# Turned first-tile blocks, token sums on VectorE, a last row block in three sums and a new stored order, in a two-block attention kernel

## The chip, the cores and the metric

The kernel runs on one core of one Trainium2 chip. The metric is the device time of one launch in microseconds (us). The names of the engines are those of the profile: PE is TensorE, DVE is VectorE, ACT is ScalarE, POOL is GpSimd and SP is SyncE. SP and ACT each have a hardware queue on which they start transfers, and POOL has a software queue.

## The reference

Two blocks share the shapes S = 2048 tokens, D = 640 features, H = 32 heads of Dh = 20, all in bf16. Block A is causal attention in a sliding window of 256 tokens, block B is linear attention with a feature map.

```python
# A
q, k, v = split_heads(x @ wqkv)
scores = einsum("bhqd,bhkd->bhqk", q, k) * Dh ** -0.5
mask = (i - j >= 0) & (i - j < 256)
p = softmax(where(mask, scores, -1e9))
a = merge_heads(einsum("bhqk,bhkd->bhqd", p, v)) @ wo
# B
phi = lambda t: where(t > 0, t + 1, exp(t)) + 1e-6
pq, pk = phi(q), phi(k)
kv = einsum("bhsd,bhse->bhde", pk, v)
z = sum of pk over the tokens s
num, den = pq @ kv, pq . z + 1e-6
b = merge_heads(num / den) @ wo
return concatenate([a, b], axis=-1)
```

The output has 2048 rows of 1280 columns, A's 640 and then B's 640.

## The kernel before

**How the order comes about.** The program records every piece of work as an operation of a planner: what it emits, on which engines it can run, what it waits for, and which shared buffer it takes. Nothing is decided at run time. The list `SEQ` (L17) holds the order: each word is an operation's number times 8 plus an engine, and `follow` (L204) emits the operations in that order. One list therefore fixes at once the order on each engine and on each queue, and the engine of each eviction that could run on ACT or on DVE.

**Shared buffers.** PSUM is split into one four-bank buffer S for scores and four one-bank buffers F0 to F3 for all other products. Four row tiles in SBUF (O0 to O3, the tile `osb`) collect rows of 640 columns before a store; a row tile comes free when its store has landed. The buffers `K0` to `K3` hold the mapped keys `pk` of the four token tiles of B and later the mapped queries `pq`; `T0` to `T3` hold the tokens of B and later `kvwo` and small sums.

**Block A.** The tokens are taken in four tiles of 512 (t = 0 to 3). A tile comes in turned, features on the partitions, by one DMA of 512 rows (`load_x`, L553). The first tile is different: its four blocks of 128 rows come in as they are (`x0n`, L1209), and PE turns each with five transposes into one PSUM buffer (L1242), which one copy moves to SBUF. `proj` makes queries and keys (512-column matmuls at L577), and POOL's DMAs at L608 and L611 regroup them into the tiles `even` and `odd`. `proj_v` makes the values (320-column matmuls, L638), and DMAs on SP's queue make the swapped copy `sw`. The weights `wq` and `wk` come in as five rows of tiles each and are copied by ACT or DVE into a padded form (L484, L486), one copy for each and a sixth for the rest.

Attention goes by score units: 16 to 24 small matmuls fill S (L708), one exponential on ACT takes S to the tile `p` (L724), DVE multiplies the edges of the window by a 0/1 strip (L736). Four units of tile 0 or five units of a later tile make a group of 8 heads; then the products with the values follow (PV, L764), 32 columns at a time, and the two result buffers are copied to `ost` and written to DRAM (L786). There are 4 groups a tile and 76 units in all. The values carry a column of ones, so the sums of the softmax come out as rows of the same product. `a_out` reads results (`oc`, L825) and sums (`osum`, L829) back, takes 1/sum as an exponential of a logarithm, scales on DVE, and multiplies by `woA` in `finish_rows` (L792): for a block of 128 rows two sums of five 320-column matmuls (L798), two copies into a row tile, and one store of 128 x 640 (L812).

**Block B.** `b_keys` makes keys from token tiles (320-column matmuls, L913), and `phi_evac` maps them: an exponential on ACT (L874), a min-and-add and a max on DVE (L878, L881). `b_sums` makes the product of tokens and mapped keys over all 16 blocks of tokens (L938), so that kv follows from it with the value weights (L1037) and, with `wo`, the matrix `kvwo` (L1055), which goes through DRAM (`kvd`, stores through row tiles). `b_z` makes the token sums of `pk`: 32 matmuls with a tile of ones of 32 columns (L974) sum over the partitions and over the four blocks of a tile; two copies and two subtractions (L986, L989) split the sums into a high and a low bf16 part, and small matmuls with a constant 1/32 turn them into columns, from which DVE makes `Zc` (L1002). `b_query` makes the mapped queries (512-column matmuls, L1107), the denominators (20 matmuls of 128 columns, L1125), their reciprocals on ACT (L1132, L1138), a spreading DMA (`recB`, L1146), the scaling on DVE (L1171), and the output by `finish_rows` with `kvwo`.

**The ends of the run.** At the start `heat` (L1185) issues 20 matmuls on a zeroed tile `warm` and four times two more. The table of ACT's functions is loaded before everything else (L505), with one small exponential (L509). At the end the last row blocks of B (named ob3.0 to ob3.3) go out. After all that a guard follows, which would compute A in a slower general form if a softmax sum left a range; here it is skipped.

## Time and profile before

| | before |
|---|---|
| median of 3 runs | 250.89 us (250.74 to 251.39) |
| the profiled run's own time | 250.49 us |
| span of the profiled execution | 248.8 us |
| busy: PE, ACT, DVE, POOL | 239.9, 200.8, 172.6, 40.4 us |
| PE busy with weight loads (beside matmuls) | 144.3 us |
| moved by DMA | 36.61 MB, mean 147 GB/s |

The span goes from the first to the last recorded instruction of the profiled execution; the run's own time holds what lies around it too. A row of the timeline has the start in us, the length, the engine, the line, the operation, out <- in by the program's names, the shape, and how often it was repeated without a break. A number in square brackets is the idle time ahead of it and what ended it. In the chain of waits each row is one step back from the last instruction. The ends of matmuls are modelled, so starts are surer than lengths.

### The profile page before, as it was taken

The numbers are of one execution on the slowest core, as the hardware profiler recorded it, in microseconds if no ns is written. First come the engines' busy times: TensorE is split into PE (matmuls) and PEld (weight loads), VectorE is DVE, ScalarE is ACT, GpSimd is POOL, SyncE is SP. The second block draws the span as 40 slices with busy tenths as digits, with TensorE's granted clock in tenths as the row PEclk, the third lists the DMA queues.
The fourth block names the chain that finished last, engine by engine and source line by source line (L and its number), as shares of the span: only waits on it lengthen the run. The fifth ranks groups of instructions, "written<-read, shape, count | busy, mean of one in ns | idle before, by whom it ended". The sixth has DMA issues, their size and how long they took to land.

```text
span 248.8 us, 9643 instructions
## 1 busy us (share of the span) xinstructions
PE 239.9 (96%) x4167; PEld 144.3 (58%) x4193; DVE 172.6 (69%) x441; ACT 200.8 (81%) x222; POOL 40.4 (16%) x93
## 2 busy tenths in 40 slices
PE   7999999999999999999999999999989999999993
PEld 6644565454655666545566666666555665565671
DVE  2553587778679978886666363369999899949740
ACT  2459898988999999988998788789999987946532
POOL 6003460063002601004078000000000000000000
PEclk9999999999999999999999999999999999999999
DMA  6999226649364759913573768863545472236433
GB/s 216 284 148 243 59 66 148 154 90 166 87 223 111 198 99 213 277 42 72 143 194 75 124 154 258 202 164 105 159 139 151 119 167 84 76 114 186 135 128 111
DMA packets 54216, 36.61 MB, mean 147 GB/s; under 512 B 34249, under 2 KB 52761, under 8 KB 54169
## 3 DMA queue, kind: packets, MB, share of 16 engines
q1 hardware_dynamic: 50537, 31.52, 49.7%
q0 software_dynamic: 2048, 2.63, 5.3%
q10 hardware_dynamic: 1584, 1.80, 2.2%
q8 instruction: 33, 0.54, 1.0%
q14 instruction: 14, 0.11, 0.2%
HBM read 13.90 MB, written 10.26 MB: 97 GB/s over the span
## 4 chain that ended last, share of the span: by engine, by line
PE 87%; ACT 6%; DVE 3%; issue 2%; DMA 1%; ACTq 0%; DVEq 0%
PE F L577 17%; PE F L798 16%; PE S L708 10%; PE F L638 9%; PE F L913 9%; PE F L938 9%; PE F L764 6%; PE F L1107 5%; ACT p L724 4%; DMA out_dram<-osb 1%; PE F L1185 1%; DVE pq L881 1%; PE F L1037 1%; ACT e L874 1%; PE F L1242 1%
## 5 line engine op out<-in xcount | busy, mean ns | idle before, releaser
L724 ACT ACTIVATE p<-S 128x2048 bf16<-128x2048 f32 x76 | 141.1, 1856 | 16.4 <-PE S L708 14.5
L736 DVE TENSOR_TENSOR p<-p,strip 128x256 bf16<-128x256 bf16 (+2 forms) x140 | 49.4, 381 | 21.1 <-ACT p L724 20.5
L874 ACT ACTIVATE e<-F 128x320 bf16<-128x320 f32 (+1 forms) x52 | 25.5, 501 | 8.3 <-PE F L1107 5.8
L638 PE MATMUL F<-wv,xT 128*128 128x320 bf16 x160 | 31.7, 300 | 0.1
L913 PE MATMUL F<-wkB,xT 128*128 128x320 bf16 x160 | 30.7, 299 | 0.2 <-issue 0.2
L798 PE MATMUL F<-woA,oc 128*128 128x320 bf16 x160 | 30.3, 300 | 0.0
L611 POOL DMA_DIRECT2D odd<-st x32 | 18.2, 573 | 69.3 <-ACT st L484 28.8
L577 PE MATMUL F<-xT,wk 128*128 128x512 bf16 x91 | 27.8, 380 | 0.3
L577 PE MATMUL F<-xT,wq 128*128 128x512 bf16 x92 | 26.9, 380 | 0.5 <-issue 0.3
L938 PE MATMUL F<-pk,xtok 128*128 128x320 bf16 x160 | 27.1, 300 | 0.0
L798 PE MATMUL F<-kvwo,pq 128*128 128x320 bf16 x160 | 25.9, 300 | 0.9 <-DVE pq L1171 0.4
L1107 PE MATMUL F<-xT,wqB 128*128 128x512 bf16 x91 | 25.4, 381 | 0.3
L486 DVE CAST ost<-F 128x512 bf16<-128x512 f32 x26 | 17.1, 685 | 10.2 <-PE F L764 10.0
L486 DVE CAST even<-F 128x512 bf16<-128x512 f32 x24 | 16.5, 688 | 8.2 <-PE F L577 7.9
L486 DVE CAST osb<-F 128x320 bf16<-128x320 f32 x33 | 15.5, 486 | 8.6 <-PE F L798 7.9
L608 POOL DMA_DIRECT2D odd<-even x32 | 16.6, 524 | 25.4 <-DVE even L486 23.2
L764 PE MATMUL F<-p,vt 64*32 64x320 bf16 (+4 forms) x720 | 20.5, 253 | 0.0
L638 PEld LDWEIGHTS <-xT 128*128 128x128 bf16 x160 | 15.1, 98 | 9.2 <-issue 1.3
L913 PEld LDWEIGHTS <-xT 128*128 128x128 bf16 x160 | 15.0, 98 | 8.9 <-issue 1.2
L764 PE MATMUL F<-p,sw 64*32 64x320 bf16 (+3 forms) x720 | 19.9, 253 | 0.2 <-DVE kvs L486 0.2
L798 PEld LDWEIGHTS <-pq 128*128 128x128 bf16 x160 | 14.9, 98 | 8.7 <-issue 1.6
L484 ACT CAST osb<-F 128x320 bf16<-128x320 f32 x31 | 12.6, 426 | 8.5 <-PE F L798 6.2
(85 smaller groups left out, 295.8 us busy)
## 6 DMA issues: line engine op xcount, KB each, us to landing
OD<-ost SPq DMA_DIRECT2D x32, 128.0 KB, 2.2
out_dram<-osb SPq DMA_DIRECT2D x24, 160.0 KB, 2.1
oc<-OD SPq DMA_DIRECT2D x4, 640.0 KB, 4.9
xtok<-in_B_x_dram SPq DMA_DIRECT2D x4, 640.0 KB, 4.5
odd<-even POOLq DMA_DIRECT2D x32, 48.0 KB, 2.9
sw<-vt SPq DMA_DIRECT2D x16, 87.0 KB, 3.1
out_dram<-osb ACTq DMA_DIRECT2D x8, 160.0 KB, 2.1
odd<-st POOLq DMA_DIRECT2D x32, 32.0 KB, 3.1
```

Source lines behind the costliest of these rows:

```text
L486: nc.vector.tensor_copy(out=dst, in_=src)
L577: nc.tensor.matmul(ps[:, a:b], lhsT=w[:, kt, i, :], rhs=xb["t"][:, kt, a:b], start=(kt == 0), stop=(kt == KT - 1))
L638: return lambda ps: nc.tensor.matmul(ps[:], lhsT=xb["t"][:, kt, bb * P : bb * P + P], rhs=rhs_(), start=(kt == 0), stop=(kt == KT - 1))
L708: nc.tensor.matmul(st["s"][64 * i : 64 * i + 64, o0 : o0 + b - a], lhsT=kb["t"][32 * j : 32 * j + Dh, sl, ko : ko + 64], rhs=qb["t"][32 * ...
L724: nc.scalar.activation(out=o_, in_=i_, func=ACT.Exp, scale=scale)
L736: nc.vector.tensor_tensor(out=x, in0=x, in1=mkv[:, None, :].to_broadcast([P, 4, 64 * w]), op=ALU.mult)
L764: nc.tensor.matmul(O[i][32 * j : 32 * j + 32, a:b], lhsT=lhsT, rhs=pb["t"][64 * i : 64 * i + 64, o0 + js * j : o0 + js * j + b - a], start ...
L798: return lambda ps: nc.tensor.matmul(ps[:], lhsT=lhs(c), rhs=rhs(c, hf), start=(c == 0), stop=(c == KT - 1))
L874: nc.scalar.activation(out=eb["t"][:, 0:n], in_=ps[:], func=ACT.Exp)
L913: return lambda ps: nc.tensor.matmul(ps[:], lhsT=xb["t"][:, kt, b * P : (b + 1) * P], rhs=R["wkB"][:, kt, hf * HALF : (hf + 1) * HALF], st ...
L938: return lambda ps: nc.tensor.matmul(ps[:], lhsT=R["xt", tb // 4][:, tb % 4, c * P : (c + 1) * P], rhs=R["pk", tb // 4][:, tb % 4, hf * HA ...
L1107: return lambda ps: nc.tensor.matmul(ps[:], lhsT=R["wqB"][:, kt, :].rearrange("p (f c) -> p c f", c=KT)[:, c, :], rhs=xb["t"][:, kt, :], s ...
```

## The change

- **First loads.** Blocks 2 and 3 of the first tile of A come in turned, by two DMA transposes of 128 rows on SP's queue, ahead of the loads of `wk` and `wq`. Blocks 0 and 1 are still turned on PE. The load of block 0 stays first on SP's queue; that of block 1 is now the first on ACT's queue, ahead of `wv0`, `wv2` and `wv4`. The first tile's SBUF layout goes by block, so that a turned block lies in one piece. The load of ACT's table and the small exponential become an operation of the order, after the copy of the first turned block. The fillers read a constant tile of ones that needs no memset; there are 18 and 16 small ones first, then two times two.
- **Token sums.** The 32 matmuls with ones and the four operations on their PSUM sums go. DVE adds up the 16 blocks of `pk` in a f32 tile of 128 x 640 (15 additions, each waiting for the one before and for its block), then splits it into high and low parts; the partitions are summed by the small matmuls that were there, with ones in place of 1/32. `Zc` moves into the tile of the parts.
- **Row tiles.** `K2` and `K3`, free of keys once the parts are made, serve as two more row tiles from there on. Until then two `hold` operations, which emit nothing, keep them taken.
- **Last row block.** ob3.2, the last in the new order, is summed in 320, 160 and 160 columns, and stored in two pieces, 480 columns and 160.
- **Weight loads of B.** `wkB`, `wvB` and `wqB` come in two transfers each, three fifths and two fifths.
- **Fillers at the first denominators.** 40 matmuls of 8 columns go ahead of the 20 of den0, into columns of the same buffer that nothing reads.
- **Order.** `SEQ` is replaced as a whole, and PV takes the pieces of its units in the order given for tile 0, in pairs of long and short for the others.

```diff
-PRM = {"sq": "SP", "dens": 4}
+PRM = {"sq": "SP", "dens": 4, "nwarm": 18, "pad": 4, "nfill": 2, "xT0": 2, "dpad": 10, "wsplit": 1, "lastb": 2}
 SEQ = [
...
+    XO = {"OK2": "K2", "OK3": "K3"} if PRM.get("xo", 1) else {}
+    pl = Planner(FB + ["S0"] + list(XO) + [f"O{i}" for i in range(PRM.get("nosb", 4))] + ["L0"])
+    held = [{} for _ in XO]
+    for g_ in held:
+        pl.op({"SP": 1}, lambda e: None, -(10 ** 8), [], name="hold", slots=(1, "O"), g=g_)
...
+    WSP = [(0, 3), (3, 5)] if PRM.get("wsplit") else [(0, 5)]
...
-        warm = mk("o", [P, NQ], BF16, "warm", tag="L0")
-        nc.vector.memset(warm[:], 0.0)
-        nc.scalar.preload_act_table_set("natural_log_exp_and_others")
+        warm = nc.const_aps.tensor(1.0, (P, P), BF16)
...
+    def row_tile(sb, name):
+        tag = sb["slot"][0]
+        return mk("over", [P, D], BF16, name, tag=XO[tag]) if tag in XO else mk("o", [P, D], BF16, name, tag="osb" + tag)
...
-        for hf in range(2):
+        cuts = [(0, HALF), (HALF, 480), (480, D)] if last else [(0, HALF), (HALF, D)]
+        for k, (a, b) in enumerate(cuts):
...
-        st = dma(lambda e: q_of(e).dma_start(out=out2[tb * P : (tb + 1) * P, col0 : col0 + D], in_=sb["t"][:]), D_STORE, -4000, ends, name="store")
+        for a, b, need in [(0, 480, ends[:2]), (480, D, ends[2:])] if last else [(0, D, ends)]:
+            st = dma(lambda e, a=a, b=b: q_of(e).dma_start(out=out2[tb * P : (tb + 1) * P, col0 + a : col0 + b], in_=sb["t"][:, a:b]), (340, 1, int(420 * (b - a) / D), 350), -4000, need, name="store")
...
-                        nc.tensor.matmul(ps[hf][32 * s : 32 * s + 32, :], lhsT=ones[:], rhs=R["pk", s][:, b, hf * HALF : (hf + 1) * HALF], start=(b == 0), stop=(b == 3), tile_position=(0, 32 * s), skip_group_check=True)
...
+        for k in range(1, NT):
+            def add(e, k=k):
+                if "zacc" not in R:
+                    R["zacc"] = mk("const", [P, D], F32, "zacc")
+                blk = lambda i: R["pk", i // 4][:, i % 4, :]
+                nc.vector.tensor_tensor(out=R["zacc"][:], in0=blk(0) if k == 1 else R["zacc"][:], in1=blk(k), op=ALU.add)
+            need = pk_ops[2 * k : 2 * k + 2] + (pk_ops[0:2] if k == 1 else [prev])
+            prev = pl.op({"DVE": 730}, add, 4000 + k, need, name=f"zs{k}")
+        def hi(e):
+            hl["t"] = mk("over", [P, 3, D], BF16, "hl", tag="T3")
+            nc.vector.tensor_copy(out=hl["t"][:, 0, :], in_=R["zacc"][:])
+        def lo(e):
+            nc.vector.tensor_tensor(out=hl["t"][:, 1, :], in0=R["zacc"][:], in1=hl["t"][:, 0, :], op=ALU.subtract)
...
-            nc.sync.dma_start(out=R["wqB"][:], in_=wBv[:, :, 0:D])
+            for a, b in WSP:
+                nc.sync.dma_start(out=R["wqB"][:, a:b, :], in_=wBv[:, a:b, 0:D])
...
+                for i in range(PRM.get("dpad", 0) if t == 0 else 0):
+                    for s_ in range(4):
+                        nc.tensor.matmul(dg["w"][32 * s_ : 32 * s_ + 32, 256:264], lhsT=ones[:], rhs=ones[:, 0:8], start=True, stop=True, tile_position=(0, 32 * s_), skip_group_check=True)
...
+                for i in range(b, b + n):
+                    nc.sync.dma_start_transpose(out=x0_tile()[:, i, :, :], in_=xA[i * P : (i + 1) * P, :])
...
+        def tables(e):
+            nc.scalar.preload_act_table_set("natural_log_exp_and_others")
+            tinyo = mk("const", [P, 1], F32, "tinyo")
+            nc.scalar.activation(out=tinyo[:], in_=tiny[:], func=ACT.Exp)
...
-            nc.sync.dma_start(out=x0n["t"][:, b, :], in_=xA[b * P : (b + 1) * P, :])
+                q_of(e).dma_start(out=x0n["t"][:, b, :], in_=xA[b * P : (b + 1) * P, :])
```

148 lines of the change are left out of this document (79 added, 69 removed), and 187 rows, old and new, of the table SEQ.

## The prediction

> **What bounds the kernel now.** I read the page first, then the timeline of PE between two score units, then the same between units late in the run.
>
> ```profile
> span 248.8 us, 9643 instructions
> PE 239.9 (96%) x4167; PEld 144.3 (58%) x4193; DVE 172.6 (69%) x441; ACT 200.8 (81%) x222; POOL 40.4 (16%) x93
> PE 87%; ACT 6%; DVE 3%; issue 2%; DMA 1%; ACTq 0%; DVEq 0%
> ```
>
> PE has 96% of the span and 87% of the chain that ended last, but a modelled matmul end hides short waits, so I test it by starts. Full-width matmuls that follow one another:
>
> ```profile
> 228.50 2.20 PE L798 MATMUL F<-kvwo,pq 128*128 128x320 bf16 x15
> 14.77 2.32 PE L577 MATMUL F<-xT,wq 128*128 128x512 bf16 x10
> ```
>
> The last of a row ends 0.30 (0.38) after it starts, as single ones do, so a 320-column matmul costs (2.20 - 0.30) / 14 = 0.136 us of PE and a 512-column one (2.32 - 0.38) / 9 = 0.216. Now one interval from a score unit (S, L708) to the next:
>
> ```profile
> 85.64 0.50 PE L708 MATMUL S<-odd 20*64 20x320 bf16 x16
> 86.08 1.67 PE L798 MATMUL F<-woA,oc 128*128 128x320 bf16 x11
> 87.58 0.84 PE L913 MATMUL F<-wkB,xT 128*128 128x320 bf16 x5
> 88.36 0.42 PE L708 MATMUL S<-odd 20*64 20x192 bf16 x16
> ```
>
> 16 x 0.136 = 2.18, plus 0.44 for S and 0.10 to turn back to row-tiled work, is 2.72: all of the interval. Counted so, with the instructions of the program's order, the intervals from the first unit (18.11) to the last (213.63) come out within about 0.1 us each, except three. So the kernel is bound by PE's own work, and by a second limit close under it, the loop of score unit and exponential:
>
> ```profile
> 181.83 0.43 PE L708 MATMUL S<-even 20*64 20x320 bf16 x24
> 182.37 1.88 ACT L724 ACTIVATE p<-S 128x2048 bf16<-128x2048 f32 x1
> 184.30 0.43 PE L708 MATMUL S<-even 20*64 20x128 bf16 x24 [0.54 <-ACT p L724]
> ```
>
> There is one S buffer, so the next unit waits for the exponential: 2.47 us per unit at least, while PE had only some 1.5 us of work here. An interval cannot shrink below that.
>
> ```profile
> core 0: us, PE busy (x) PEld busy (x) DVE busy (x) ACT busy (x) POOL busy (x), PEclk, DMA share, GB/s
> 113.04:165.88 52.84, 52.66 (x1123) 33.10 (x1125) 28.61 (x72) 44.89 (x40) 13.27 (x27) 1.00 0.65 159
> 165.88:176.38 10.50, 10.30 (x179) 6.48 (x181) 9.32 (x25) 9.50 (x9) 0.00 (x0) 1.00 0.40 114
> 176.38:184.30 7.92, 6.86 (x173) 4.15 (x173) 7.74 (x20) 7.82 (x9) 0.00 (x0) 1.00 0.50 164
> ```
>
> From 113 to 166 PE is full and DVE has 24 us free; from 176 to 184 DVE and ACT are full and PE waits. Those are the three exceptions: 7.92 us for about 6.1 us of PE work, 1.8 us lost.
>
> **The change part by part.** The whole order is replaced, so I counted each interval of the new order in the same way.
>
> *The start.*
>
> ```profile
> 1.50 2.74 PE L1185 MATMUL F<-warm 128*128 128x128 bf16 x24 [1.50 <-DVE tiny L507]
> 4.81 0.49 DVE L486 COPY xT<-F 128x640 bf16<-128x640 bf16 x1 [3.36 <-PE F L1242]
> 5.66 2.47 PE L638 MATMUL F<-wv,xT 128*128 128x320 bf16 x16
> 7.97 0.44 PE L1242 MATMUL F<-ident,x0n 128*128 128x128 bf16 x5
> 8.24 0.43 PE L638 MATMUL F<-wv,xT 128*128 128x320 bf16 x2
> 8.52 0.44 PE L1242 MATMUL F<-ident,x0n 128*128 128x128 bf16 x5
> 8.79 2.20 PE L638 MATMUL F<-wv,xT 128*128 128x320 bf16 x15
> 10.80 1.22 DVE L486 COPY wk<-wkn 128x512 bf16<-128x512 bf16 x5 [0.52 <-DMA wkn<-in_A_wqkv_dram]
> 9.86 4.51 SPq L553 DMA_TRANSPOSE xT<-in_A_x_dram  x1
> ```
>
> Blocks 2 and 3 of the first tile come turned by DMA: two groups of transposes leave PE, 8.24 - 7.97 and 8.79 - 8.52, so -0.54. Two fillers now stand between the first value matmuls: +0.1. The second block's load goes first on ACT's queue instead of second on SP's, three wv loads follow it there, and the filler no longer waits for a memset (1.50), so the first value matmul (5.66) can come earlier; but the first copy moves from DVE (0.49) to ACT, which by its 426 ns for 320 columns and 584 for 512 needs an estimated 0.7, behind three more DMA issues and a table load. I take -0.2. Against it: the two turned loads stand on SP's queue before all ten wk and wq loads. A 512-row turn holds SP for 4.51 us, a quarter of that is 1.1, so two take 2.3 where two plain loads took 0.9, and DVE already waited 0.52 for wk. I charge nothing more than the gain I held back above. Start: -0.6, bounds -1.1 (first matmul 0.6 earlier) and +0.8 (wk late by the 1.4 of issue, less the saved 0.6).
>
> *Token sums.*
>
> ```profile
> 166.23 1.27 PE L974 MATMUL F<-pk,ones 128*32 128x320 bf16 x32
> 167.44 1.27 PE L1107 MATMUL F<-xT,wqB 128*128 128x512 bf16 x4
> L881 DVE SCALAR_TENSOR_TENSOR pq<-F,e 128x512 bf16<-128x512 f32 x20 | 13.7, 689 | 0.6
> L881 DVE SCALAR_TENSOR_TENSOR pk<-F,e 128x320 bf16<-128x320 f32 x32 | 15.6, 490 | 0.9
> L1002 DVE TENSOR_TENSOR Zc<-blk,zs 128x640 bf16<-128x640 bf16 x1 | 0.8, 826 | 0.0
> ```
>
> PE loses 32 matmuls, 167.44 - 166.23 = -1.2. DVE gains 15 adds of 640 f32 elements. From 490 to 689 ns for 192 more is 1.04 ns an element; from 512 to 640 that makes 0.82, as the 640-wide product at L1002 has. I take 0.8 each, 12 us in all (0.5 if they ran like the bf16 products, 1.0 if f32 in SBUF costs more), less the four copies that leave. They lie in 113 to 166, where 24 us are free. The cover is thinnest where seven stand in a row, 5.6 us, ahead of the last six masks of tile 2, group 3: counted from the exponentials they depend on, the masks end about 0.3 us after the PV there could start. +0.1; without cover, 12 us.
>
> [...]
>
> *The loop's floor.* With 1.8 us less PE work before the late stage, three intervals hold 2.31, 2.33 and 2.34 us where about 2.43 is the least: +0.3.
>
> *The late stage* (units from 174 to 192). Per unit ACT has the same exponentials; other ACT work is nearly equal, and it set the pace before: 0. Forty 8-column fillers join the first denominator group, 10 to 25 ns each (weight loads of 20 such take 0.31): 0.4 to 1.0, partly in PE's wait; with two sums and the split copies DVE has about 1 us more in a stage where it is full. Together +0.3, bounds -1.0 and +1.5.
>
> *Halved weight loads:* one more SP issue each, 0.5 us, hidden by loads that are due 5 us later. *Row tiles, last block:*
>
> ```profile
> 218.97 0.48 PE L1125 MATMUL F<-pq,Zc 128*32 128x128 bf16 x20
> 222.71 0.60 ACT L874 ACTIVATE e<-F 128x512 bf16<-128x512 f32 x1 [2.41 <-PE F L1107]
> 225.89 0.58 PE L798 MATMUL F<-kvwo,pq 128*128 128x320 bf16 x3 [0.42 <-DVE pq L1171]
> 240.34 3.43 DMA out_dram<-osb
> 243.84 0.43 ACT osb L484
> 244.32 0.85 PE F L798 x5
> 245.20 0.42 ACT osb L484
> out_dram<-osb ACTq DMA_DIRECT2D x8, 160.0 KB, 2.1
> recB<-recS SPq DMA_DIRECT2D x16, 32.0 KB, 1.9
> ```
>
> The first three rows are the timeline, the next four the chain, the last two the DMA issues. At 240.34 a store holds the row tile that an eviction needs, four PSUM buffers fill, and PE waits some 0.5 before 244.32. Six row tiles instead of four end that: -0.5. The other tail wait (225.89) stays: the new order has 4.0 us of PE work from the denominator to the first product that needs it, where the old had 5.9; but its scale multiply stands two DVE results earlier. I get a wait of 0.9 where 0.6 was. Smaller tail waits even out. Tail: -0.4, bounds -1.2 and +0.8. At the end the last eviction is 160 columns, an estimated 0.29 instead of 0.42, and the last store 40 KB: by 2.1 and 1.9 above, -0.1. End: -0.2.
>
> Sum: -0.6 - 1.2 + 0.1 + 0.3 + 0.3 - 0.4 - 0.2 = -1.7. The profiled run took 250.49, that is 1.7 outside its span, and 0.40 under the median of 250.89. Off the median, with rounding, 249.1.
>
> **The rivals.** *All stalls go* (247.3): the 1.8 us of the late stage vanish too. For it: they come from DVE's order (copies of kvwo, masks), and that is new. Against: ACT's sum there is as long as before.
>
> *The turned blocks come late* (250.6): DMA is the limit of the first 10 us, SP's queue is 1.4 us longer, and wk was just in time; then start is +0.8 and more, and only the token sums pay.
>
> *VectorE becomes the bound* (slower, 252.3): the seven adds hold the masks, PV comes late, and two adds and two splits follow into the full stage. Eleven operations at c us each cost 11c - 8.8 of delay; 0.96 is break-even, at 1.1 it is 3.3. For it: no row shows an f32 add in SBUF. Against: no 640-wide row is above 0.826.
>
> *PE's clock comes up late* (250.8): the 24 fillers start 0.107 apart ((2.74 - 0.29) / 23), the transposes at 7.97 0.055, so PE runs at half rate until about 5.7. The new filler ends near 3.4 and PE may idle until the first block lands; if full rate came one filler's length (2.7) plus that later, 3.4 us of work at half rate lose 1.7. The profile's granted clock is 1.00 throughout and shows none of it. [...]
>
> **How the numbers follow.** Forecast 0.52 (248.1 to 250.2), all stalls go 0.18, late blocks 0.13, late clock 0.08, VectorE 0.09. What a measurement can tell from no change is 0.3%, 0.75 us: faster is below 250.14, slower above 251.64. Faster takes 0.50 + 0.18 + 0.06 of the late cases: 0.76; slower 0.09 and a little of the late ones: 0.10; the rest 0.14. Range 247.4 to 251.0: it leaves out the VectorE case and the lower part of the first rival.
>
> **What would show it.** First value matmul near 5.4 and first score unit near 17.5; no idle before the first key matmul. No matmuls from the ones tile on 640-wide keys; 15 adds of about 0.8; the unit before PV of tile 2, group 3 not longer than 2.8. Units from 174 to 192 still paced by the exponential. PE without a wait in its last 5 us, and the last eviction near 0.3. I am wrong if the first unit is not earlier than 18.1, if adds take 1 us, or if units of 113 to 166 exceed their matmul sum.

## The result and the profile after

| | before | after |
|---|---|---|
| median | 251.06 us (250.21 to 252.14, 18 runs) | 252.58 us (251.22 to 253.50, 18 runs) |
| profiled run, and its span | 250.49, 248.8 us | 252.12, 250.6 us |
| ratio after / before | | 1.0059, 95% interval [1.0040, 1.0078] |

The changed kernel is slower by 0.6%. The forecast of 249.1 was wrong in sign, and the range up to 251.0 did not hold the time. Runs in which the chip was in its slower state (one of a_w26d7, two of a_w26code, and one of the kernel before beside a_dpad6) are left out of the medians and ranges below.

First the page of the changed kernel: span, engines, one DMA queue, the chain that ended last.

```profile
span 250.6 us, 9689 instructions
PE 240.0 (96%) x4181; PEld 144.1 (57%) x4206; DVE 184.1 (73%) x452; ACT 202.3 (81%) x223; POOL 40.5 (16%) x92
...
q8 instruction: 34, 0.56, 1.0%
...
PE 87%; DVE 4%; ACT 3%; DMA 2%; issue 2%; ACTq 0%; DVEq 0%
```

Nothing there says what went wrong: PE has the same share, DVE has the 11.5 us of additions it was given, and the span is 1.8 us longer. So I cut the span by the starts of score units, which both kernels share (unit S1.2.3 is the fourth of group 2 of tile 1, counted from 0), and set the stretches side by side. The last two columns are experiments that are told below.

| stretch (us) | before | after | fuller start | fuller start, fewer fillers |
|---|---|---|---|---|
| to the first unit S0.0.0 | 18.11 | 18.55 | 17.70 | 17.58 |
| to S3.0.0 | 145.29 | 145.09 | 145.08 | 145.19 |
| to S3.0.3 (token sums were here) | 7.91 | 7.66 | 7.66 | 7.67 |
| to S3.2.3 (late stage) | 25.97 | 27.08 | 26.56 | 26.36 |
| to S3.3.4, the last unit | 16.35 | 15.99 | 15.99 | 16.35 |
| to the start of the last matmul | 31.23 | 31.07 | 31.05 | 31.05 |
| to the end of the span | 3.94 | 5.16 | 4.66 | 3.50 |

The last row is good to 0.05, because the pages give the span to 0.1. Three stretches got longer: the start (+0.44), the late stage (+1.11) and, least expected, the end (+1.22), where PE has nothing left to do. Each column is one execution, and the start differs between executions: three other kernels with the fillers and first loads of before (b_dpad4, b_noguard, b_sums2) have their first unit at 18.32 to 18.72. So the +0.44 alone shows little; the medians of the experiments have to carry that part.

*The end.* The last eviction and the last store on ACT, in the timeline of the changed kernel:

```profile
245.71 0.29 ACT L491 CAST osb<-F 128x160 bf16<-128x160 f32 x1 [1.12 <-PE F L813]
246.03 0.34 ACTq L828 DMA_DIRECT2D out_dram<-osb  x1
```

The eviction takes the 0.29 that was forecast. The store after it holds 40 KB instead of 160 KB. Yet the span ends 4.6 us after the store was issued; before it was 3.2 after this one:

```profile
245.65 0.34 ACTq L812 DMA_DIRECT2D out_dram<-osb  x1
```

The DMA view of the last stretch of each kernel shows what the engines moved, in 40 slices; first before, from 243.7 to 249 (0.13 us a slice):

```profile
DMA  0000000000200599711899999710200200000000
GB/s 0 0 0 0 0 0 0 0 0 0 62 0 0 193 377 348 261 49 68 290 396 348 329 377 386 261 29 0 62 0 0 62 0 0 0 0 0 0 0 0
```

then after, from 245.4 to 251 (0.14 us a slice):

```profile
DMA  0089999977988220000220000000000000000000
GB/s 0 27 293 357 366 375 329 347 229 238 460 268 215 53 59 0 0 0 0 59 65 7 14 7 14 18 7 0 0 0 0 0 0 0 0 0 0 0 0 0
...
q14 instruction: 3, 0.02, 1.7%
q8 instruction: 1, 0.02, 1.6%
```

Before, full rate ends in slice 25 and what follows are two isolated reads. After, full rate ends at about 247.2, and from 248.3 to 249.2 a trickle of 7 to 18 GB/s comes after it, some 67 x 0.14 = 9.4 KB. The trace's packets give it exactly: 7,684 bytes on SP's queue and 2,564 on ACT's, which is one sixteenth of 120 KB and of 40 KB (and 4 bytes each). One of the 16 pieces of each store is late by 2 us; the other 15 had landed by 247.56 and 247.73, the last ones at 249.51 and 249.67. And the queue lines show what else was moved meanwhile: three reads of 8,192 bytes on q14, which before has in its last stretch too, and one read of 16,384 bytes on q8. It starts at 246.87 and takes 1.4 us, when all but three of PE's recorded instructions have begun. I take it for a block of PE's own program: PE begins some 250 recorded instructions between two such reads on average, and in the experiments the reads move when PE's instructions alone are changed. Before had 33 such reads, the last at 241.31; here there are 34.

What is read there? PE's last matmuls are followed by the guard: a flag is loaded and compared, and a branch passes over instructions that are not executed. The read comes only 65 recorded instructions after the one ahead of it (241.89), so it does not look like the next block in order. My reading is that the branch brings it on: whether the place behind the guard lies in a block that PE already holds would depend on how long its program is, to a few instructions. The trace does not tell what a read is for. PE's branch starts at 245.46 and takes 0.36 us (244.92 and 0.24 before), and PE's first instruction behind the guard starts at 246.02, 0.84 ahead of the read; so PE did not stand at the branch until the block had come. What speaks for the reading is told below: the read comes or stays away with the length of the program, and the kernel without the guard has none at its end.

*The start.* PE's timeline of the changed kernel:

```profile
1.08 2.08 PE L1207 MATMUL F<-const-bfloat16-1.0 128*128 128x128 bf16 x18 [1.08 <-PEq L1516]
3.09 0.30 PE L1210 MATMUL F<-const-bfloat16-1.0 128*32 128x32 bf16 x16
3.86 1.25 PE L1291 MATMUL F<-ident,x0n 128*128 128x128 bf16 x10 [0.47 <-POOL vt L541]
4.90 0.42 PE L1207 MATMUL F<-const-bfloat16-1.0 128*128 128x128 bf16 x2
5.36 0.71 PE L646 MATMUL F<-wv,xT 128*128 128x320 bf16 x2
5.86 0.42 PE L1207 MATMUL F<-const-bfloat16-1.0 128*128 128x128 bf16 x2
6.52 5.06 PE L646 MATMUL F<-wv,xT 128*128 128x320 bf16 x32 [0.23 <-DMA wv<-in_A_wqkv_dram]
```

The first value matmul starts at 5.36, as forecast. But PE idles 0.47 us ahead of the first transposes, and at 6.52 it waits for wv. In that row the matmuls start 0.267 apart up to 7.54 and 0.136 from then on. Before, the step to full rate came at 5.93. So half rate lasts 1.6 us longer in these two executions. In the chain of waits wv stands ahead of the values:

```profile
1.96 4.51 DMA wv<-in_A_wqkv_dram
...
6.52 5.06 PE F L646 x32
```

*Where the forecast held.* The additions on DVE (groups by line), and two rows of PE's tail:

```profile
L993 DVE TENSOR_TENSOR zacc<-zacc,pk 128x640 f32<-128x640 f32 x14 | 11.5, 823 | 0.3
```

```profile
225.64 0.31 PE L813 MATMUL F<-kvwo,pq 128*128 128x320 bf16 x1 [0.62 <-DVE pq L1193]
...
239.36 6.32 PE L813 MATMUL F<-kvwo,pq 128*128 128x320 bf16 x50
```

Fourteen of the fifteen additions stand in that group, at 0.823 us each, where 0.8 was taken and 0.96 was break-even. From 239.36 on 50 matmuls run without a break: the wait ahead of 244.32 is gone.

The late stage, in the window that was shown of before (columns as there):

```profile
core 0: us, PE busy (x) PEld busy (x) DVE busy (x) ACT busy (x) POOL busy (x), PEclk, DMA share, GB/s
176.38:184.30 7.92, 7.14 (x184) 4.46 (x191) 7.84 (x21) 7.86 (x9) 0.00 (x0) 1.00 0.85 151
```

DVE and ACT are as full as they were, 7.84 and 7.86 of 7.92.

### The profile page after: what moved, and what is told of

The parts are those of the page before. It is cut to its first block, busy times and chain, and to the rows that moved or that the text cites. A ratio compares the mean times of both kernels' runs of the same rounds, so it can differ in the third digit from the quotient of the medians.

```text
span 250.6 us, 9689 instructions
## 1 busy us (share of the span) xinstructions
PE 240.0 (96%) x4181; PEld 144.1 (57%) x4206; DVE 184.1 (73%) x452; ACT 202.3 (81%) x223; POOL 40.5 (16%) x92
## 4 chain that ended last, share of the span: by engine, by line
PE 87%; DVE 4%; ACT 3%; DMA 2%; issue 2%; ACTq 0%; DVEq 0%
PE F L813 18%; PE F L584 16%; PE S L717 10%; PE F L954 9%; PE F L929 9%; PE F L774 7%; PE F L647 7%; PE F L1123 6%; PE F L646 2%; ACT p L733 2%; DMA wv<-in_A_wqkv_dram 2%; DVE pq L897 1%; ACT e L890 1%; DVE p L745 1%; PE F L1146 1%
## 5 line engine op out<-in xcount | busy, mean ns | idle before, releaser
L954 PE MATMUL F<-pk,xtok 128*128 128x320 bf16 x160 | 28.3, 300 | 0.0
L584 PE MATMUL F<-xT,wq 128*128 128x512 bf16 x96 | 27.5, 380 | 0.3 <-issue 0.2
L584 PE MATMUL F<-xT,wk 128*128 128x512 bf16 x88 | 26.6, 380 | 0.5 <-ACT e L890 0.2
L813 PE MATMUL F<-kvwo,pq 128*128 128x320 bf16 (+1 forms) x165 | 25.9, 296 | 0.7 <-DVE pq L1193 0.6
L647 PE MATMUL F<-wv,xT 128*128 128x320 bf16 x120 | 26.4, 300 | 0.1
L493 DVE CAST even<-F 128x512 bf16<-128x512 f32 x27 | 18.3, 688 | 7.2 <-PE F L584 6.9
L491 ACT CAST osb<-F 128x320 bf16<-128x320 f32 (+1 forms) x33 | 13.7, 421 | 9.5 <-PE F L813 7.9
L894 DVE TENSOR_SCALAR e<-e 128x320 bf16<-128x320 bf16 (+1 forms) x52 | 13.5, 260 | 10.1 <-ACT e L890 9.2
L929 PEld LDWEIGHTS <-xT 128*128 128x128 bf16 x160 | 15.1, 98 | 8.9 <-issue 1.5
L493 DVE CAST osb<-F 128x320 bf16<-128x320 f32 (+1 forms) x32 | 14.9, 480 | 6.7 <-PE F L813 4.9
```

Source lines behind the costliest of these rows:

```text
L493: nc.vector.tensor_copy(out=dst, in_=src)
L584: nc.tensor.matmul(ps[:, a:b], lhsT=w[:, kt, i, :], rhs=rhs, start=(kt == 0), stop=(kt == KT - 1))
L647: return lambda ps: nc.tensor.matmul(ps[:], lhsT=xb["t"][:, kt, bb * P : bb * P + P], rhs=rhs_(), start=(kt == 0), stop=(kt == KT - 1))
L813: return lambda ps: nc.tensor.matmul(ps[:], lhsT=lhs(c), rhs=rhs(c, a, b), start=(c == 0), stop=(c == KT - 1))
L929: return lambda ps: nc.tensor.matmul(ps[:], lhsT=xb["t"][:, kt, b * P : (b + 1) * P], rhs=R["wkB"][:, kt, hf * HALF : (hf + 1) * HALF], st ...
L954: return lambda ps: nc.tensor.matmul(ps[:], lhsT=R["xt", tb // 4][:, tb % 4, c * P : (c + 1) * P], rhs=R["pk", tb // 4][:, tb % 4, hf * HA ...
```

## The experiments

Each was compared with the kernel before on the same chip; those medians lay between 250.73 and 251.01. "Fillers" at the first denominators are the matmuls of 8 columns. The count of PE's weight loads on the page (4193 before, 4206 after) serves as the length of PE's program; the records of matmuls, 4167 and 4181, are 26 and 25 fewer.

### The start: keep PE busy, or not

*a_warm26*, the changed kernel with 26 full and 8 small fillers at the start instead of 18 and 16, the same number of instructions.

```diff
-"nwarm": 18, "pad": 4
+"nwarm": 26, "pad": 2
```

> The changed kernel with 26 full and 8 small fillers at the start instead of 18 and 16: as many PE instructions, but PE has work until the first block of x lands at 3.85. Theory (clock): in the changed kernel PE stands idle from 3.4 to 3.86 and runs at half rate until 7.75 (before: until 5.9); with the gap closed the full rate comes about 4.3 us after the first filler, at 5.4 to 5.8, the first score unit at 17.9 instead of 18.55, time about 252.0. Rival (late weights alone, the wv load that lands at 6.47, sets the start): full rate still only after 7.5, first score unit at 18.4 or later, time 252.5.

Measured: 250.95 us (250.24 to 251.65, 12 runs), ratio 0.9996 [0.9980, 1.0013]. That is further than the 252.0 expected. PE's timeline:

```profile
1.08 2.93 PE L1207 MATMUL F<-const-bfloat16-1.0 128*128 128x128 bf16 x26 [1.08 <-PEq L1516]
3.94 0.24 PE L1210 MATMUL F<-const-bfloat16-1.0 128*32 128x32 bf16 x8
4.12 0.92 PE L1291 MATMUL F<-ident,x0n 128*128 128x128 bf16 x10
...
6.22 4.51 PE L646 MATMUL F<-wv,xT 128*128 128x320 bf16 x32
```

No idle row up to the transposes, full rate from 4.6, and 32 value matmuls in 4.51 instead of 5.06. The kernel wins 252.58 - 250.95 = 1.63 us, though the block read at the end is there (at 244.85). Its runs spread over 1.4 us, those of after over 2.3. Of the win the two profiles show 0.85 in the start; the other stretches that got shorter, by 0.5 each, hold nothing that was edited, so how much of the 1.63 belongs to the start alone is not settled. b_gap bounds it from the other side.

*b_gap*, the mirror: the kernel before with 8 full fillers and 12 small ones instead of 20 full ones.

```diff
-PRM = {"sq": "SP", "dens": 4}
+PRM = {"sq": "SP", "dens": 4, "nwarm": 8}
...
+            for i in range(3 if n > 4 else 0):
+                for s_ in range(4):
+                    nc.tensor.matmul(psum(g)[32 * s_ : 32 * s_ + 32, 0:32], lhsT=warm[:, 0:32], rhs=warm[:, 0:32], start=True, stop=True, tile_position=(0, 32 * s_), skip_group_check=True)
```

> The kernel before with 8 full and 12 small fillers at the start instead of 20 full ones: as many PE instructions, but PE stands idle for about 1.3 us ahead of the first transposes. Theory (clock): full rate comes 3.4 to 4 us after the transposes begin at 4.03, at 7.4 to 8.0 instead of 5.9; 7 to 8 value matmuls run at 0.267 instead of 0.136, first score unit at 18.9 to 19.2, time 251.8 to 252.1. Rival (the gap at the start has no such effect; the scatter of the changed kernel is from its loads alone): 250.9.

Measured: 252.49 us (251.82 to 252.92, 7 runs), ratio 1.0059 [1.0037, 1.0082]: a loss as large as that of the whole change, made in the kernel before by fewer full fillers at the start alone.

```profile
3.43 0.71 PE L1245 MATMUL F<-ident,x0n 128*128 128x128 bf16 x5 [0.16 <-DMA x0n<-in_A_x_dram]
4.54 0.72 PE L1245 MATMUL F<-ident,x0n 128*128 128x128 bf16 x5 [0.40 <-DMA x0n<-in_A_x_dram]
...
5.63 3.59 PE L638 MATMUL F<-wv,xT 128*128 128x320 bf16 x16
```

The same 16 value matmuls, from 5.63 here and 5.66 before, take 3.59 instead of 2.47. Half rate lasts to 8.24, 4.8 after the first transposes where 3.4 to 4 were expected, and the first unit stands at 19.19 instead of 18.11. The other 0.6 of this profile's loss stands between the last unit and the last matmul (31.84 instead of 31.23), a stretch that takes 30.66 to 32.31 among the kernels that keep the order of before. The granted clock over the first 18 us is 1.00 in the profiles of before, after, a_warm26, a_dpad6, a_w26d7b and b_gap; only the spacing shows the rate. In a_warm26 PE works from 1.08 without a gap, and full rate comes at 4.6, 3.5 later. a_w26d0 (told below) has 26 full fillers and no gap either, yet its transposes and its value matmuls up to 10.5 go at half rate.

```profile
1.08 2.93 PE L1207 MATMUL F<-const-bfloat16-1.0 128*128 128x128 bf16 x26 [1.08 <-PEq L1516]
3.96 1.25 PE L1291 MATMUL F<-ident,x0n 128*128 128x128 bf16 x10
...
6.82 5.07 PE L646 MATMUL F<-wv,xT 128*128 128x320 bf16 x23 [0.43 <-DMA wv<-in_A_wqkv_dram]
```

Its first unit stands at 20.08. Profiles with the start of before differ too: full rate comes at 5.93 in before, 6.80 in b_noguard and 7.07 in b_sums2, without an idle row in any of them, and by 5.3 in b_dpad4, right behind an idle 0.54. So the profiles do not show that an idle gap alone decides when full rate comes. What the medians of a_warm26 and b_gap show is that the fillers at the start move the time by 1.5 to 1.6 us.

### The end: the branch and its block

*a_dpad6*, the changed kernel with 24 fillers at the first denominators instead of 40.

```diff
-"dpad": 10
+"dpad": 6
```

> The changed kernel with 24 fillers at the first denominators instead of 40: PE's program is 32 instructions shorter, nothing else changes. Theory (code block): in the changed kernel a 16 KB block of PE's program is read at 246.87 us, just as the last two stores run; it occupies one of the 16 DMA engines, and one sixteenth of each of these stores lands 2 us after the rest (249.51 and 249.67 against 247.6). With 32 instructions less that read is not reached before the end: from the last eviction's end to the span's end 3.2 us instead of 4.6, time about 251.0 (1.4 less for the end, 0.2 for the fillers). Rival (the two-piece store, or the many stores on ACT's queue, is what makes the end long): the end stays 4.6, time 252.4.

Measured: 251.59 us (249.26 to 252.91, 12 runs), ratio 1.0010 [0.9983, 1.0036]. PE has 16 matmuls fewer (4190 weight loads), no block is read after the last matmul has started, and the end takes 3.56 us instead of 5.16. The late stage takes 26.34 instead of 27.08. The start of the profiled run is worse than that of after, though nothing in it was changed:

```profile
3.74 1.25 PE L1291 MATMUL F<-ident,x0n 128*128 128x128 bf16 x10 [0.35 <-DMA x0n<-in_A_x_dram]
...
6.89 4.96 PE L646 MATMUL F<-wv,xT 128*128 128x320 bf16 x18 [0.73 <-DMA wv<-in_A_wqkv_dram]
```

18 value matmuls, 0.267 apart, in 4.96 us: half rate to beyond the end of this view (full rate comes at 12.6), and the first unit at 21.12. Over the four profiles with 18 full fillers and the gap, full rate comes at 7.7 (after and a_dpad0), 8.8 (a_noguard) and 12.6; the spread of 3.6 us among the runs is of that size.

*b_dpad4*, the kernel before with 16 such fillers.

```diff
+                for i in range(4 if t == 0 else 0):
+                    for s_ in range(4):
+                        nc.tensor.matmul(dg["w"][32 * s_ : 32 * s_ + 32, 256:264], lhsT=ones[:], rhs=ones[:, 0:8], start=True, stop=True, tile_position=(0, 32 * s_), skip_group_check=True)
```

> The kernel before with 16 fillers of 8 columns at the first denominators: PE's program is 32 instructions longer, nothing else changes. Theory (code block): the next 16 KB block of PE's program is now read while the last stores run; the span's end comes 1 to 2 us later after the last eviction (4.2 to 5 instead of 3.2), time about 252.6 (1.4 for the end, 0.2 for the fillers). Rival: the end stays 3.2 us, time 251.2.

Measured: 250.71 us (250.36 to 251.36, 12 runs), ratio 0.9982 [0.9960, 1.0005]. A miss in the time, for 252.6 was expected. The read is there (at 245.50, 4209 weight loads), and the end takes 4.43 instead of 3.94. But the block read ahead of it moved from 241.31 to 239.80, away from the stores that a row tile waited for, and from the last unit to the last matmul it took 30.66 instead of 31.23. Whether the one led to the other this profile does not show: among the kernels that keep the order of before that stretch takes 30.66 to 32.31.

*a_dpad0*, no fillers at the denominators, and *a_w26d0*, none there and none of the small ones at the start (with 26 full ones).

```diff
-"nwarm": 18, "pad": 4, "dpad": 10
+"nwarm": 18, "pad": 4, "dpad": 0
...
+"nwarm": 26, "pad": 0, "dpad": 0
```

> The changed kernel without the 40 fillers at the first denominators: 80 PE instructions fewer. Theory (code block): the block read at 241.89, which delays a sixteenth of the stores issued at 240.01 and 240.39 to 244.1 and 244.5 and so holds two evictions at 244.2, moves past the last product too; no eviction waits for a store after 240, and the end is 3.2 us; with 0.5 for the fillers the time is 249.2 to 250.3. Rival (stores as such are slow): evictions still wait 1.5 us at 244, time about 252.1.

> The changed kernel with 26 full fillers at the start, no small ones, and none at the first denominators: 72 PE instructions fewer than the mixed version and 16 fewer than the version whose block was read just at its end. Theory (code block): no block is read in the last 12 us, end 3.5, and the late stage is 0.2 shorter: 249.2 to 249.5. Rival (the block before is still read at the end): end near 4.8, time 250.4.

Measured: 251.70 us (250.62 to 252.67, 12 runs), ratio 1.0028 [1.0007, 1.0049]; and 250.97 us (250.44 to 253.09, 13 runs), ratio 0.9992 [0.9971, 1.0012]. Both miss what was expected, for both have the read (at 245.62 and 247.93) and long ends, 4.93 and 5.19. So a shorter program is not safe: now, it seems, the block before has not been read when the branch comes (there are 33 reads, as many as in the kernels without one at the end). In the time the read hardly shows between a_dpad0 and a_dpad6, which has none: 251.70 against 251.59. In a_dpad0 and in b_dpad4 it starts 0.5 to 0.6 us after the last matmul, in the other six kernels 0.8 to 1.6; whether that is why it costs less there was not tested. The late stage of both takes 26.25, so the 40 fillers cost 27.08 - 26.25 = 0.8 there, and the rest of the growth, 0.3, is the order's.

*a_w26d7*: both remedies, a fuller start and 28 fillers at the denominators, for a program of 4194 weight loads; and the same kernel again as *a_w26d7b*, beside *a_w26d8*, which has four tiny fillers more and is otherwise the same.

```diff
-"nwarm": 18, "pad": 4, "dpad": 10
+"nwarm": 26, "pad": 2, "dpad": 7
...
+"nwarm": 26, "pad": 2, "dpad": 8
```

> The changed kernel with 26 full and 8 small fillers at the start and 28 fillers at the first denominators instead of 40 (24 PE instructions fewer than with 40). What the first runs showed goes in: closing PE's idle gap at the start was worth 1.6 us (250.95), and in every profile so far a read of a 16 KB block of PE's program falls in the last stores (last matmul to span end 4.4 to 5.2 us) or not (3.6 and 3.9); the program that is 24 instructions shorter doesn't reach the last block. Theory (code block): last matmul to span end near 3.6, time 249.5 to 249.9, below both kernels. Rival (the end varies for another reason, the median doesn't follow the code): 250.6 to 250.9, only the 12 fillers less.

> The mixed version once more, on a chip with its neighbour of 8 more instructions. Theory (jump): no block of PE's program is read at the last jump, last matmul to span end 3.5, time 249.4 to 249.8. Rival (the first result was luck of that chip): 250.5 or more.

> The mixed version with 32 instead of 28 fillers at the first denominators: 8 PE instructions more and nothing else. In the profiles so far PE's program, counted with the skipped guard, had 8530 to 8538 rows where no block was read at the end, and 8544 or more, or 8482 or less, where one was. Theory (jump): PE's last instruction jumps over the guard to the end of the program; with 8546 rows the target lies one 16 KB block further, the block is read then, a sixteenth of the last stores lands 2 us late; last matmul to span end 4.5 to 5, time 250.6 to 251.0. Rival (fillers cost by their own time): 249.6 to 249.7.

Measured: 249.53 us (249.16 to 251.10, 9 runs), ratio 0.9949 [0.9928, 0.9971], and again 249.51 (249.13 to 250.23, 6 runs), ratio 0.9943 [0.9929, 0.9958]. With four matmuls more, 251.08 (250.15 to 252.73, 12 runs), ratio 1.0006 [0.9987, 1.0026]. 1.57 us for four matmuls of 8 columns. The last eviction and store of each, then what the DMA engines moved (from 244.8 to 249 in the first, 0.105 us a slice, from 244.5 to 250 in the second, 0.14); first a_w26d7b:

```profile
245.14 0.29 ACT L491 CAST osb<-F 128x160 bf16<-128x160 f32 x1 [1.76 <-PE F L813]
245.46 0.34 ACTq L828 DMA_DIRECT2D out_dram<-osb  x1
```

```profile
GB/s 390 305 61 0 0 61 305 378 341 329 147 37 229 329 357 262 241 179 6 0 0 0 0 0 0 78 78 0 0 0 0 0 0 0 0 0 0 0 0 0
```

and a_w26d8:

```profile
244.82 0.29 ACT L491 CAST osb<-F 128x160 bf16<-128x160 f32 x1 [1.76 <-PE F L813]
245.14 0.34 ACTq L828 DMA_DIRECT2D out_dram<-osb  x1
```

```profile
GB/s 382 131 0 0 177 391 344 261 40 357 342 263 215 99 0 0 0 14 7 74 67 19 14 0 0 0 0 0 0 0 0 0 0 0 0 0 0 0 0 0
...
q8 instruction: 1, 0.02, 1.2%
```

a_w26d8 issues its last store 0.3 us earlier and ends 0.9 later (249.2 against 248.3): the trickle and the block read are back.

*a_w26code*, as a_w26d7 with 12 matmuls of 8 columns in the first of the later fillers: the length of after again, but with none of the added matmuls in the late stage.

```diff
+            for i in range(12 if key == 10 ** 7 else 0):
+                nc.tensor.matmul(psum(g)[:, 0:8], lhsT=warm, rhs=warm[:, 0:8], start=True, stop=True)
```

> The mixed version (26 full and 8 small fillers, 28 at the first denominators; 249.53) with 12 matmuls of 8 columns added to the first filler after the transposes, where PE waits 0.6 us for a copy anyway: only the length of PE's program grows, by 24 instructions, to that of the version with 250.95. Theory (code block): the last 16 KB block is read at the end again, last matmul to span end 4.5 to 5 instead of 3.5, time 250.5 to 250.9. Rival (the 1.42 us between the two versions came from the 12 fillers at the denominators): the end stays 3.5, time 249.5 to 249.7.

Measured: 252.30 us (251.33 to 254.02, 7 runs), ratio 1.0054 [1.0026, 1.0082]. The read is at 248.79, the end takes 5.31, the late stage 26.36 as in a_w26d7. The 2.8 us over a_w26d7 are more than the read costs elsewhere, and more than was expected. In the profiled run, of 253.96, 3.0 us were lost between S2.1.2 and S2.1.3, behind late DMAs of `osum` and `oc`; whether the other runs had that stall is not known.

*b_w24* and *b_w24s*: the same in the kernel before. Both have fillers on the constant tile, 24 of them first. b_w24 has two in each of the later fillers as before, b_w24s one (the last edit), four matmuls less.

```diff
-        warm = mk("o", [P, NQ], BF16, "warm", tag="L0")
-        nc.vector.memset(warm[:], 0.0)
+        warm = nc.const_aps.tensor(1.0, (P, P), BF16)
...
-        heat(2, 10 ** 7 + i)
+        heat(1, 10 ** 7 + i)
```

> The kernel before with the constant tile of ones for its fillers (no memset to wait for) and 24 of them instead of 20, so that PE works from about 1.1 us on without a gap. Theory (clock): full rate at about 4.6 instead of 5.9, second block's transposes and the first value matmul faster, first score unit at 17.8 to 18.0, time 250.5 to 250.8, and less scatter. Rival (the start before is bound by its loads alone): 251.0, first score unit at 18.1.

> The kernel before with 24 fillers on the constant tile at the start, as in the run of 252.93, but with one instead of two matmuls in each of its four later fillers: 8 PE instructions fewer, 8536 rows, as many as before the change. Theory (jump): no block is read at the end, last matmul to span end 3.8 instead of 6.0, time 250.3 to 250.8. Rival (the constant tile or the longer heat-up itself costs the 1.9 us): 252.5 or more.

Measured: 252.93 us (252.58 to 253.83, 6 runs), ratio 1.0073 [1.0055, 1.0091]; and 250.78 (250.04 to 251.91, 11 runs), ratio 0.9999 [0.9984, 1.0014]. 2.15 us for four matmuls, or 1.9 by the ratios, since the two ran beside different runs of before, with the program at 4197 and 4193 weight loads. b_w24 was expected to win and lost. b_w24s, which reads no block, has full rate from 4.2 and is no faster than before: its value matmuls then wait 0.40 for wv at 6.59. From 246.3 to 253 (0.17 us a slice) in b_w24:

```profile
GB/s 0 0 0 0 267 359 321 321 449 260 168 352 336 77 49 0 0 0 57 8 8 8 15 23 31 23 0 0 0 0 0 0 0 0 0 0 0 0 0 0
...
q8 instruction: 1, 0.02, 1.6%
```

The same trickle; its stores are of 160 KB, and it is longer: the end takes 6.01 us, that of b_w24s 3.92.

*a_noguard* and *b_noguard*: the guard and its branch left out of the changed kernel and of the kernel before.

```diff
-PRM = {
+PRM = {"noguard": 1,
```

> Leaves out of the changed kernel the guard at the end of the program (a flag is loaded and compared, and a branch passes over instructions that are never executed). Theory (the jump): without the branch no block of PE's program is read while the last stores are under way; from the start of the last matmul to the span's end 3.5 us instead of 5.16, time 251.0 to 251.2. Rival (the longer program or the fillers themselves cost the time, the read is a bystander): 5.16 stays, time 252.4 to 252.6.

> Leaves the same guard out of the kernel before, which read no block at its jump. Theory (the jump): nothing to win, the end stays at 3.8 to 3.9 us after the start of the last matmul, time 250.8 to 251.0. Rival (the guard costs time in itself, read or not): as much faster as the changed kernel without it, 249.4 to 249.7.

Measured: 250.14 us (249.28 to 251.36, 12 runs), ratio 0.9977 [0.9956, 0.9997]; and 250.85 (250.19 to 251.87, 12 runs), ratio 1.0007 [0.9991, 1.0022]. The DMA view of a_noguard from 244.2 to 250 (0.145 us a slice):

```profile
GB/s 26 62 291 380 327 124 18 0 291 380 335 124 0 0 0 185 380 371 345 362 353 239 186 364 296 241 71 0 0 0 0 0 0 0 0 0 0 0 0 0
...
q10 hardware_dynamic: 589, 0.55, 27.7%
q1 hardware_dynamic: 288, 0.29, 14.8%
```

No instruction read of any queue, no trickle, and an end of 3.15 us. By the ratios the changed kernel wins 1.0059 - 0.9977 = 0.8%, 2.1 us, more than the 1.4 to 1.6 expected; one profile has 2.0 of it in the end (5.16 to 3.15). The kernel before wins nothing, with an end of 3.79: it read no block of PE's there. This rules out the rival that the guard costs time in itself, and that the 40 fillers, which a_noguard keeps (late stage 26.96), cost the time at the end.

Over all 20 profiles, those with a block read behind the branch (each time with three of PE's recorded instructions left) end 4.43 to 6.01 us after the last matmul's start, and those without 3.15 to 4.10. The read comes with 4158 to 4166 and with 4197 to 4209 weight loads (a_noguard, which has no branch, aside), and not with 4189 to 4194.

### Single parts of the change

*b_sums* and *b_sums2*: the token sums on DVE alone, in the order of before. The first makes up for the lost matmuls of PE with small fillers at the start (17 full and 36 small), the second with 28 at the denominators, its start as before.

```diff
-                        nc.tensor.matmul(ps[hf][32 * s : 32 * s + 32, :], lhsT=ones[:], rhs=R["pk", s][:, b, hf * HALF : (hf + 1) * HALF], start=(b == 0), stop=(b == 3), tile_position=(0, 32 * s), skip_group_check=True)
...
+        for k in range(1, NT):
+            def add(e, k=k):
...
+                nc.vector.tensor_tensor(out=R["zacc"][:], in0=blk(0) if k == 1 else R["zacc"][:], in1=blk(k), op=ALU.add)
```

> The kernel before with only the token sums moved: 32 matmuls go, 15 additions of about 0.82 us go to DVE where it stood idle, and the heat-up at the start has 17 full and 36 small matmuls instead of 20 full ones, so that PE's program keeps its length. By the prediction's terms -1.2 for the matmuls and +0.1 for the additions: 249.8 to 250.0. Rival (the 1.2 us is given back: the units after the sums meet the loop of score unit and exponential, or DVE's longer chain to the first query products holds them): 250.6 to 251.0.

> The kernel before with the token sums on DVE, the heat-up at the start left as it was (20 full fillers), and 28 fillers at the first denominators so that PE's program stays in the harmless lengths (8528 rows). In the earlier run the three units after the sums took 7.57 us together instead of 7.91, while 32 matmuls of 1.2 us had gone: each unit still needs its score and exponential. Theory (loop): only 0.3 is won, the fillers cost 0.15, time 250.7 to 250.9. Rival (the prediction's term): 1.1 is won, time 250.0 to 250.2.

Measured: 252.23 us (251.00 to 253.50, 10 runs), ratio 1.0051 [1.0029, 1.0073]; and 250.83 (249.98 to 252.90, 12 runs), ratio 1.0007 [0.9986, 1.0029]. b_sums is outside both of its expected ranges, and its profile tells of the start instead: full rate does not come before 10.1 us, and the first unit stands at 20.83. Whether its 36 small fillers are the reason is not shown, since a_w26d0, with full ones alone, is as late. In both, S3.0.0 to S3.0.3, where the 1.2 us of matmuls were, takes 7.57 and 7.58 instead of 7.91: 0.34 won. PE's timeline of b_sums2 there:

```profile
166.84 1.27 PE L1104 MATMUL F<-xT,wqB 128*128 128x512 bf16 x5
...
168.91 0.43 PE L707 MATMUL S<-even 20*64 20x320 bf16 x24 [0.79 <-ACT p L723]
...
171.58 0.43 PE L707 MATMUL S<-even 20*64 20x128 bf16 x24
```

The unit at 168.91 now waits 0.79 for the exponential of the unit before it. PE lost 32 matmuls there and waits in their place. The 28 fillers take the gain back, with a late stage of 26.68 against 25.97.

*b_turn* and *b_turn2*: blocks 2 and 3 turned by DMA, alone, in the order of before; with 18 full fillers and 12 small ones, and with 20 full ones and 8 fillers at the denominators.

```diff
+    def em_t(e):
+        for i in (2, 3):
+            nc.sync.dma_start_transpose(out=x0_tile()[:, i, :, :], in_=xA[i * P : (i + 1) * P, :])
...
-    for b in range(4):
+    for b in range(2):
```

> The kernel before with only blocks 2 and 3 of the first tile turned by DMA on SP's queue, in place of their plain loads and 10 transposes on PE; the heat-up has 18 full and 12 small matmuls, so that PE's program keeps its length. By the prediction's terms -0.54: first score unit at 17.6, time 250.4. Rival (the turned loads make the value weights or wk late): first score unit at 18.1 to 19, time 250.9 to 251.8.

> The kernel before with blocks 2 and 3 turned by DMA, as in the earlier run, but with its 20 full fillers and no small ones (8 fillers at the first denominators keep PE's program within 4 instructions of its length). In the earlier run the small fillers ahead of the transposes kept PE at half rate until 7.3. If that was all that hid the gain: full rate at about 5.9, first score unit at 17.6, time 250.4 to 250.6. Rival (the turned loads are late themselves): first score unit at 18 or later, time 250.8 to 251.0.

Measured: 250.80 us (250.19 to 251.31, 12 runs), ratio 0.9993 [0.9978, 1.0009]; and 251.12 (249.94 to 252.42, 12 runs), ratio 0.9998 [0.9977, 1.0019]. No difference from before, where 0.54 of transposes left PE. In b_turn half rate lasts to 7.17 and in b_turn2 to about 6.2, where before it was 5.93 and other executions of the same start had up to 7.07, and in b_turn2 the second block comes late (0.56 of idle at 5.33). So neither shows what the turned loads would bring at full rate, nor that the small fillers kept b_turn at half rate; that stays open.

## Why the prediction was wrong, and where it was right

*"End: -0.2" is the step that failed.* It counted the shorter eviction and the smaller store, and both came as counted: without the block read the end takes 3.43 to 3.56 us in the changed kernels, 0.4 to 0.5 less than before's 3.94. What it left out is that the change makes PE's program longer by 13 matmuls and their weight loads (4193 to 4206), that a block of 16,384 bytes is then read at the end, by my reading because of the guard's branch, and that one sixteenth of each of the last two stores then comes some 2 us after the rest. The term is +1.2 in the profiled run, and 1.6 to 2.1 in the three comparisons that turn on the read (a_w26d8, b_w24, a_noguard); in b_dpad4 and a_dpad0 the median shows next to nothing of it, and why is open. Nothing that was quoted of before could show it: the chain of waits there ends in a store, and the page counts no branch as work.

*"Start: -0.6" is the second.* It came out at +0.44 in the profile. What then happened stood in a rival at 0.08, "PE's clock comes up late". The rival's price came out (1.7 forecast; a_warm26 wins 1.63 and b_gap loses 0.6%, 1.5 us, of which 0.85 and 1.08 stand in the start of the profiles), and so did its condition. Its assumption that full rate would come 3.4 later was my estimate, from the filler's 2.7 and the idle time, and the profiles do not bear it out: it came 1.6 later in the profile of after, and at 7.7 to 12.6 over the four with that start. Its premise, that the fillers end near 3.4 while the first block lands later, could be worked out from the rows, and it held: idle from 3.39 to 3.86. A premise that follows from the order deserved more than 0.08.

252.58, less 1.63 for the start, less 1.57 for the read, is 249.4, and a_w26d7, which mends both, measured 249.53 and 249.51. That sum is no test in itself, since its steps lead through a_warm26 and a_w26d8 to a_w26d7. The other way, over a_dpad6, gives by the ratios 1.2 for the read and 1.6 for the start, each good to about 0.8; within that the two add up. The forecast of 249.1 was for a kernel without either, and is within 0.4 of that one. Part of that is luck: in the profile of a_w26d7 the token sums with the floor bring -0.3 where -0.8 was forecast, the tail -0.2 where -0.4 was, and the end -0.4 where -0.2 was.

Set beside the forecast, the two profiles of before and after differ from it by 1.4 in the end, 1.0 in the start, 0.8 in the late stage and 0.35 in the token sums with the floor.

The other steps:

- *The parts of the start.* The first value matmul came at 5.36 as forecast (near 5.4). With 26 full fillers the first unit stands at 17.58 to 18.56 in five profiles (the latest is a_w26d7b, where wv landed late) and at 20.08 in a_w26d0, against 18.11 before. The two turned loads held SP's queue for 2.79 us, where 2.3 was taken. The limit behind is wv and not wk, which the sum had in view: the key matmuls did not wait.
- *Token sums, -1.2 and +0.1.* The additions took 0.823 us. Between the first and the last unit PE's records are the same in number by kind, except for the 32 matmuls that go, the 1.2 that was counted, and the 40 fillers that come.
- *Floor, +0.3, was mis-sized.* The intervals over the same stretch went from 195.52 to 195.82, so waits and fillers there grew by some 1.5. In b_sums2, 1.2 - 0.34 = 0.86 come back as a wait for the exponential within three units.
- *Late stage, +0.3.* +0.3 from the order (25.97 to 26.25 without fillers), and the 40 fillers add 0.3 (a_warm26) to 0.8 (after): +1.1 in the changed kernel, inside the bound of +1.5. The units are still paced by ACT and DVE.
- *Tail, -0.4.* From S3.2.3 to the last matmul it takes 47.06 instead of 47.58, -0.5. The row tiles do what they should, and the wait at 225.64 is there, with 0.62 where 0.9 was forecast. It also gave shelter: in the changed kernel the last sixteenth of a store issued at 240.01 landed only at 244.1, after the block read at 241.89, and PE did not stop.
- *VectorE becomes the bound:* ruled out by 0.823. *The turned blocks come late:* no loss in b_turn and b_turn2.
- *Two slips in the sums.* The parts given for "faster" add up to 0.74 and not 0.76, and 250.89 less 1.7 is 249.2. Neither bears on the argument.

The version that beats both kernels is a_w26d7, by 0.5% against before. Its length was chosen so that no block is read at the end, and none was; it is the fuller start and that length, not a new part, that turn the change into a gain.

## What to carry to other kernels

When a change alters the count of instructions, look at the instruction reads of the profile (the queue lines, then the DMA view of the last microseconds) before and after: a block read while the last stores are in flight can cost more than the edit saves (here 1.6 to 2.1 us in three comparisons, next to nothing in two kernels), and a few tiny instructions more or less tell it apart (four matmuls of 8 columns, 1.57 us). At the start of a kernel, judge PE's rate by the spacing of equal matmuls, take an idle gap before the first loads land as a possible cost of its own, and judge it by medians, because one profile's start can be off by 2 us and more (first unit at 18.55 in after, at 21.12 in a_dpad6, with the same start). Work taken from PE where it runs close to the pace of another engine can be worth far less than its own time: of 1.2 us of matmuls 0.34 was won here.

## What the hardware showed that I had not expected

- A 16,384-byte read at the end takes 0.95 to 1.75 us in the eight profiles that have one, and it goes with exactly one sixteenth of the stores then in flight moving late: in the changed kernel 7,684 and 2,564 bytes, about 2 us after the rest, in b_dpad4 less than 1. That both pass through the same DMA engine is what the sixteenth suggests; the trace does not name the engine. In the time it is 1.6 to 2.1 us in three comparisons, and next to nothing in b_dpad4 and a_dpad0.
- The 8 KB instruction reads on another queue, two or three at the end of the kernels with the guard (three in after, two in b_w24), cost nothing that could be measured: b_noguard, without them, is at 1.0007 of before.
- When PE's full rate comes differs widely between profiles: between 5.3 and 7.07 us in four profiles with the start of before, 4.1 to 6.0 in five with 26 full and 8 small fillers, and 10.5 with 26 full ones alone (a_w26d0), in none of these with an idle gap ahead of the first transposes. Why is open.
